# Attention and a squared-ReLU FFN on one core: the second FFN matrix product with seven block products in place of eight

## The chip, the cores and the metric

The kernel runs on one core of one Trainium2 chip. The metric is the device time of one execution in microseconds (us). TensorE (PE in the profile) multiplies, VectorE (DVE), ScalarE (ACT) and GpSimd (POOL) work element by element, and SyncE (SP) issues every DMA of this kernel.

## The reference

Eight batches, twelve heads, 448 positions, head size 64, all in float32. The attention output, 3584 rows of 768, goes through an FFN.

```python
q_n, k_n = rmsnorm(q, g_q), rmsnorm(k, g_k)
scores = q_n @ k_n.T / sqrt(64)
attn = softmax(scores) @ v              # per batch and head
x = attn as (3584, 768)
h = x @ w_in                            # w_in  (768, 2048), float64 in memory
g = s * relu(h) ** 2 + b
out = (g @ w_out).astype(float32)       # w_out (2048, 768), float64 in memory
```

## The kernel before

**Numbers in two parts.** TensorE takes its operands as fp32r. To keep float32 accuracy, each operand is held as a rounded part (hi) and a remainder (lo), and a product is three matmuls: hi by hi, hi by lo, lo by hi. The weights arrive as float64; L130 to L138 put the two 32-bit words of each number together into float32 with four DVE operations and one ACT square, and L141 and L144 split that into hi and lo.

**The attention loop** (L612 to L655) is written as slots. One slot (s_) handles one chunk of 128 keys of one head: `score_t` (2 matmuls), `score` for the chunk ten slots ahead (1 matmul, followed on DVE by `maximum`), `weigh` for the chunk two slots behind (3 matmuls, or 2 for the last chunk of a head). A pair of heads takes 8 slots, a batch 48. All engines get their instructions in exactly the order in which they are written. On DVE, `split_e_lo` (L453, tile al) of a slot must be done before `weigh` of the next slot starts; it also frees a PSUM bank that a later `score` (L375, tile sh) takes. Other work hangs on slot numbers in the table `jobs`: the norm (L317), scaling (L338), the divisor (L495) and so on of pairs to come.

**FFN1** (h = x w_in) runs inside this loop as filler: from slot START = 8 of the next batch on, six matmuls a slot, exactly 48 slots for the 288 matmuls of a batch. Its input tiles x are split in slots 7 to 12 of the batch (`split_x`, L517). What is left of the last batch runs after the loop, in the first part of FFN2's code (L722 to L753), 18 matmuls a step. There w_out is loaded, converted and split in 32 pieces (`load_double`, L120), into the room of w_in. The rectified h goes to DRAM (r_d).

**FFN2** (out = g w_out) has 28 tiles of 128 rows. `squares` (L672) loads a tile of h with all 2048 columns, squares it on ACT (L685), applies s and b on DVE (L686), and splits it (L690, L691). `ffn_out` (L694) runs 16 chunks times three matmuls times two column halves: 96 matmuls of 384 columns per tile (L703), 2688 in all, into two PSUM banks.

Of the kernel before, what the change touches and what calls it, by code (L numbers as in the profile page):

```python
# [20 lines left out]

LEAST = (1 + 1 / 8) * 2.0 ** (0x70 - 127)

START = 8

AHEAD = 10

# [6 lines left out]
TURNED = 10  # L34

PLAIN = 10

GAP = 2

# [2 lines left out]
def attention_then_relu2_ffn(  # L42
# [49 lines left out]
    NS = 4  # L92
    FS = DF // NS
    WI = 512
    WO = 384
    W = 8
    NSLOT = W * NPAIR

# [10 lines left out]
    warm = cpool.tile([P, 1], F32, name="warm")  # L109

    r_d = [dpool.tile([NFC, P, SEQ], F32, name=f"r_d{b}") for b in range(B)]
    z_d = [dpool.tile([2, SEQ], F32, name=f"z_d{p}") for p in range(NPAIR)]
    i_d = [dpool.tile([2, 2 * SEQ], F32, name=f"i_d{p}") for p in range(NPAIR)]

# [2 lines left out]
        bank = free.pop(0)  # L117
        return ps.tile([P, 512], F32, tag=bank, name=name), bank

    def load_double(room, dst_hi, dst_lo, src, apart=False, rest=None):  # L120

        w, words, m = room
        nc.sync.dma_start(w.rearrange("p n t -> p (n t)"), src)
        yield
        a = words()
# [9 lines left out]
        V.scalar_tensor_tensor(af, m.bitcast(F32), LEAST * LEAST, af, ALU.is_ge, ALU.mult)  # L138
        for _ in range(GAP):
            yield  # L140
        S.copy(dst_hi, af)  # L141
        if apart:
            yield
        (rest or G).tensor_tensor(dst_lo, af, dst_hi.bitcast(F32), ALU.subtract)  # L144
        yield

    w_in32 = w_in.bitcast(I32)
    w_out32 = w_out.bitcast(I32)
    whi, wlo, ohi, olo = ([None] * NS for _ in range(4))
# [12 lines left out]
    def parts_of_w_out():  # L162
        n = NFC // NS
        for i in range(NS):
            ohi[i] = wpool.tile([P, n, DM], F32R, tag=f"wh{i}", name=f"woh{i}")
            olo[i] = wpool.tile([P, n, DM], F32R, tag=f"wl{i}", name=f"wol{i}")
            for f in range(n):
                r0 = (i * n + f) * P
                for c0 in range(0, DM, WO):
                    c = slice(c0, c0 + WO)  # L170
                    src = w_out32[r0 : r0 + P, 2 * c0 : 2 * (c0 + WO)]
                    yield ohi[i][:, f, c], olo[i][:, f, c], src

# [43 lines left out]
    with tc.tile_pool(name="apool", bufs=1) as ap:  # L217
# [280 lines left out]
        def divide(p, step):  # L498
# [24 lines left out]
        def pieces():  # L523
            for i, (hi, lo, src) in enumerate(parts_of_w_in()):
# [38 lines left out]
        for p in range(NPAIR):  # L563
# [26 lines left out]
            at(s0 + 16, divide, p, 2)  # L590
            at(s0 + 18, divide, p, 3)
# [5 lines left out]
        for i, s_ in enumerate(PACE):  # L597
            for n in range(5):
                at(s_ + n, convert, i, n)
            at(s_ + 3, load_piece)  # L600

        def within(i):
            return 0 <= i < NSLOT
# [53 lines left out]
            keep_r()  # L657


    with tc.tile_pool(name="opool", bufs=2) as op:  # L660

        def pieces():
            for i, part in enumerate(parts_of_w_out()):
                w = op.tile([P, WO, 2], I32, tag="w64", bufs=4, name=f"w64o{i}")
                m = op.tile([P, WO], F32, tag="wm", bufs=2, name=f"wmo{i}")

                def words(i=i):
                    return op.tile([P, WO], I32, tag="wa", bufs=6, name=f"wao{i}")

                yield load_double((w, words, m), *part, apart=True, rest=V)  # L670

        def squares(t):  # L672
            r = op.tile([P, NFC, P], F32, tag="r2", bufs=2, name=f"r2_{t}")
            t0 = t * P
            while t0 < (t + 1) * P:
                b, off = divmod(t0, SEQ)
                n = min((t + 1) * P - t0, SEQ - off)
                o = t0 - t * P
                nc.sync.dma_start(
                    r[:, :, o : o + n],  # L680
                    r_d[b][:, :, off : off + n].rearrange("f p t -> p f t"),
                )
                t0 += n
            yield
            S.activation(r, r, AF.Square)  # L685
            V.tensor_scalar(r, r, sb_s, sb_b, ALU.mult, ALU.add)  # L686
            yield
            gh = op.tile([P, NFC, P], F32R, tag="gh", bufs=3, name=f"gh{t}")
            gl = op.tile([P, NFC, P], F32R, tag="gl", bufs=3, name=f"gl{t}")
            S.copy(gh, r)  # L690
            V.tensor_tensor(gl, r, gh.bitcast(F32), ALU.subtract)  # L691
            yield gh, gl

        def ffn_out(ts, gs):  # L694
            n = NFC // NS
            pos = [[psum(f"po{t}_{e}") for e in range(2)] for t in ts]
            for i in range(NS):
                for (gh, gl), po in zip(gs, pos):
                    for f in range(n):
                        fc = i * n + f  # L700
                        for m, (x, w) in enumerate(((gh, ohi[i]), (gh, olo[i]), (gl, ohi[i]))):
                            for e in range(2):
                                T.matmul(  # L703
                                    po[e][0][:, :HALF],
                                    x[:, fc, :],
                                    w[:, f, e * HALF : (e + 1) * HALF],
                                    start=fc == 0 and m == 0,
                                    stop=fc == NFC - 1 and m == 2,
                                )
            for t, po in zip(ts, pos):  # L710
                ot = op.tile([P, DM], F32, tag="ot", name=f"ot{t}")
                S.copy(ot[:, :HALF], po[0][0][:, :HALF])
                V.tensor_copy(ot[:, HALF:], po[1][0][:, :HALF])
                free.extend(bank for _, bank in po)
                nc.sync.dma_start(out[t * P : (t + 1) * P, :], ot)

        first = [squares(t) for t in range(3)]
        gs = []
        pieces = pieces()


        later_by = 2  # L722
        with tc.manual_schedule(engines=ORDERED - {ENGINE.SP}):
            waiting = []
            todo = list(islice(pieces, 2))
            for g in todo:
                next(g)
            for m in range(NFC + later_by):
                filler(NCC * 3)
                now, todo = todo, list(islice(pieces, 2))  # L730
                for g in todo:
                    next(g)
                if m in (1, 2, 3):
                    next(first[m - 1])
                old = waiting[:2] if m >= later_by else []
                waiting = waiting[len(old) :]
                for step in range(4):
                    for g in now:
                        next(g)
                    if step == 0:  # L740
                        rectify()
                        keep_r()
                        for g in old:
                            for _ in range(GAP):
                                next(g)
                    if step == 2:
                        for g in old:
                            next(g)
                waiting += now
                if m in (6, 8, 10):  # L750
                    next(first[(m - 6) // 2])
                if m in (7, 9, 11):
                    gs.append(next(first[(m - 7) // 2]))  # L753
        ffn_out([0, 1, 2], gs)
        for t in range(3, NT // P):
            *_, g = squares(t)
            ffn_out([t], [g])


_INS = ["moe_w_in", "moe_w_out", "moe_s", "moe_b"]  # L760
# [41 lines left out]
```

## Time and profile before

| | us |
|---|---|
| median of 3 runs | 1480.66 (1477.99 to 1481.07) |
| the profiled execution | 1479.64 |
| its span, first to last instruction | 1477.8 |
| PE busy, share of the span | 1443.6, 98% |
| DVE busy | 863.5, 58% |
| ACT busy | 799.8, 54% |
| POOL busy | 687.8, 47% |
| granted TensorE clock, mean | 0.994 of full speed |

Matmuls are pipelined, so a busy PE is not by itself a PE at its peak. The distance between the starts of matmuls tells how fast it goes. The execution has three stretches: an opening of about 217 us, in which PE often waits; the attention loop with filler up to about 955 us; and the FFN2 stretch, whose matmuls run from 1006 us to 1473 us.

### The profile page before, as it was taken

What the parts mean: (1) busy time and instruction counts of PE and PEld (TensorE: products, weight loads), DVE (VectorE), ACT (ScalarE), POOL (GpSimd) and SP (SyncE); (2) the same over time, 40 slices, a digit from 0 to 9 for tenths busy, and PEclk for the clock granted to TensorE, in tenths of its full rate; (3) what the DMA queues carried; (4) which work ended last, traced back from release to release, by engine and by line L of the source; (5) the groups of instructions that cost most, each with busy time, mean ns of one, the idle gap of its engine ahead of it and who ended that gap; (6) DMA issues with size and microseconds to landing.
All of it is one profiled execution on the core that took longest, in us unless ns stands there. A gap on an engine that the chain in (4) does not pass through costs nothing.

```text
span 1477.8 us, 21404 instructions
## 1 busy us (share of the span) xinstructions
PE 1443.6 (98%) x7360; PEld 1328.2 (90%) x7360; DVE 863.5 (58%) x1347; ACT 799.8 (54%) x1466; POOL 687.8 (47%) x559
## 2 busy tenths in 40 slices
PE   7998999999999999999999999999999999999998
PEld 5666779899899899899899999899999999999998
DVE  6888896766766766766676764289522222222210
ACT  5876566766766767766766766456332222222210
POOL 7797787777777767767777763100000000000000
PEclk8999999999999999999999999999999999999999
DMA  4545776666666666666666652288323323233200
GB/s 130 142 129 155 215 215 194 183 196 189 194 197 173 184 194 196 180 202 182 181 200 190 193 177 68 98 280 251 116 81 90 104 82 79 80 96 99 79 22 33
DMA packets 215100, 223.46 MB, mean 151 GB/s; under 512 B 75536, under 2 KB 192272, under 8 KB 214992
## 3 DMA queue, kind: packets, MB, share of 16 engines
q1 hardware_dynamic: 214992, 222.10, 51.4%
q8 instruction: 58, 0.95, 0.3%
q14 instruction: 50, 0.41, 0.1%
HBM read 169.87 MB, written 40.81 MB: 143 GB/s over the span
## 4 chain that ended last, share of the span: by engine, by line
PE 82%; DVE 8%; DMA 3%; issue 2%; POOL 2%; ACT 2%; SPq 0%; POOLq 0%; ACTq 0%; DVEq 0%
PE po L703 31%; PE ph L185 24%; PE av L472 13%; PE sh L375 5%; PE st L413 4%; PE st L416 4%; DMA w64o<-in_dram 1%; DMA w64i<-in_dram 1%; DVE nmx L386 1%; DVE kq L338 1%; PE tk L253 1%; DVE x L521 1%; DVE wao L133 1%; DVE ssq L317 1%; DVE al L453 1%
## 5 line engine op out<-in xcount | busy, mean ns | idle before, releaser
L185 PE MATMUL ph<-x,wih 128*128 128x448 f32 x1536 | 492.7, 367 | 5.6 <-ACT x L520 3.1
L185 PEld LDWEIGHTS ph<-x,wih 128*128 128x128 f32 x1536 | 288.5, 189 | 35.4 <-issue 5.3
L386 DVE TENSOR_REDUCE nmx<-sh 112x1 fp32r<-112x448 f32 x384 | 237.2, 620 | 114.0 <-PE sh L375 111.3
L185 PE MATMUL ph<-x,wil 128*128 128x448 f32 x768 | 291.1, 379 | 0.0
L432 ACT ACTIVATE st<-st 128x448 f32<-128x448 f32 (+1 forms) x304 | 159.4, 524 | 222.0 <-PE st L416 219.3
L703 PE MATMUL po<-woh,gh 128*128 128x384 f32 x896 | 227.6, 334 | 1.0 <-ACT gh L690 1.0
L703 PE MATMUL po<-woh,gl 128*128 128x384 f32 x896 | 227.4, 334 | 0.0
L703 PE MATMUL po<-wol,gh 128*128 128x384 f32 x896 | 227.3, 334 | 0.0
L472 PE MATMUL av<-ah,vs 128*128 128x448 f32 x608 | 173.9, 367 | 3.6 <-DVE al L453 3.6
L440 ACT CAST ah<-st 128x448 fp32r<-128x448 f32 (+1 forms) x304 | 162.6, 535 | 1.6
L703 PEld LDWEIGHTS po<-woh,gh 128*128 128x128 f32 x896 | 161.7, 188 | 1.4 <-ACT gh L690 1.3
L375 PE MATMUL sh<-ka,qa 128*112 128x448 f32 x384 | 147.9, 387 | 14.3 <-DVE ka L265 7.2
L703 PEld LDWEIGHTS po<-woh,gl 128*128 128x128 f32 x896 | 161.7, 188 | 0.1
L703 PEld LDWEIGHTS po<-wol,gh 128*128 128x128 f32 x896 | 161.6, 188 | 0.0
L453 DVE TENSOR_TENSOR al<-st,ah 128x448 fp32r<-128x448 f32 x228 | 139.6, 612 | 36.9 <-ACT ah L440 24.1
L185 PEld LDWEIGHTS ph<-x,wil 128*128 128x128 f32 x768 | 144.6, 188 | 16.5 <-issue 5.3
L413 PE MATMUL st<-qa,ka 128*128 128x448 f32 (+1 forms) x384 | 158.0, 411 | 1.0 <-ACT e L428 0.9
L685 ACT ACTIVATE r<-r 128x2048 f32<-128x2048 f32 x28 | 53.7, 1919 | 170.3 <-DMA r<-r_d 170.3
L513 POOL TENSOR_TENSOR u<-uz,zb 64x448 f32<-64x448 f32 x96 | 123.0, 1281 | 40.0 <-DMA zb<-z_d 36.4
L416 PE MATMUL st<-qb,kb 128*128 128x448 f32 (+1 forms) x384 | 140.8, 367 | 0.0
L686 DVE TENSOR_SCALAR r<-r,sb_s,sb_b 128x2048 f32<-128x2048 f32 x28 | 37.6, 1344 | 172.3 <-ACT r L685 172.3
L375 PEld LDWEIGHTS sh<-ka,qa 128*112 128x112 f32 x384 | 107.4, 281 | 27.0 <-issue 5.3
(75 smaller groups left out, 2120.5 us busy)
## 6 DMA issues: line engine op xcount, KB each, us to landing
kq<-in_dram SPq DMA_DIRECT2D x76, 448.0 KB, 5.1
rb<-i_d SPq DMA_DIRECT2D x76, 448.0 KB, 6.0
r_d<-r SPq DMA_DIRECT2D x128, 224.0 KB, 3.1
r<-r_d SPq DMA_DIRECT2D x24, 1024.0 KB, 5.9
raw<-in_dram SPq DMA_DIRECT2D x38, 448.0 KB, 5.0
w64i<-in_dram SPq DMA_DIRECT2D x24, 512.0 KB, 4.6
w64o<-in_dram SPq DMA_DIRECT2D x32, 384.0 KB, 4.4
kb<-ka SPq DMA_DIRECT2D x96, 112.0 KB, 2.9
```

The costliest lines, as they stand in the source:

```text
L185: T.matmul(ph[:, :SEQ], w[:, cc, f0 : f0 + P], xs[b, cc][:, part, :], start=cc == 0 and m == 0, stop=cc == NCC - 1 and m == 2,)
L375: T.matmul(sh[:QC, :SEQ], qa[p % 2][:, a].rearrange("k (p c) -> k c p", c=NQ)[:, c], ka[p % 2][:, a], start=True, stop=True,)
L386: V.tensor_reduce(out=nmxs[p][:, c : c + 1], in_=sh[:QC, :SEQ], op=ALU.max, axis=AX.X, negate=True)
L413: T.matmul(st[:rows, :SEQ], ka[n][:, keys], qa[n][:, q], start=True, stop=False)
L416: T.matmul(st[:rows, :SEQ], kb[n][:, keys], qb[n][:, q], start=False, stop=True,)
L432: S.activation(st[:rows, :SEQ], st[:rows, :SEQ], AF.Exp)
L440: S.copy(ah[:rows], sts[i][0][:rows, :SEQ])
L453: V.tensor_tensor(al, st[:rows, :SEQ], ah[:rows].bitcast(F32), ALU.subtract)
L472: T.matmul(av[:, :SEQ], x, a, start=kc == 0 and m == 0, stop=kc == 3 and m == len(todo) - 1,)
L513: G.tensor_tensor(u[a], uzs.pop((p, j))[a], zb[a], ALU.mult)
L685: S.activation(r, r, AF.Square)
L703: T.matmul(po[e][0][:, :HALF], x[:, fc, :], w[:, f, e * HALF : (e + 1) * HALF], start=fc == 0 and m == 0, stop=fc == NFC - 1 and m == 2,)
```

## The change

FFN2 is computed by Strassen's scheme in its form with 7 products. Two row tiles (256 rows), the two halves of the 2048 inner indices, and the two halves of the 768 columns form 2 by 2 blocks. Seven products of (128 x 1024) by (1024 x 384) replace eight; each is 24 matmuls of 384 columns. There are 14 groups of 7 products, 2352 matmuls. The left sums (`sum1` to `sum4`) and the output sums (`settle`) are made on DVE. The four right sums need w_out as float32 before it is split: in batches 2 to 7 of the attention loop, four pieces per batch, at slots 16, 24, 32 and 40 of the batch (`PACE_OUT`), are loaded, converted and summed, and the blocks (b_d) and sums (t_d) are written to DRAM. After the loop they are loaded in chunks and split in place. START goes from 8 to 9, the divisor of the last pair of a batch is one slot earlier (`soon`), and the tile u has 5 buffers, not 6.

```diff
-START = 8
+START = 9
+PACE_OUT = tuple(48 * b + 16 + 8 * i for b in range(2, 8) for i in range(4))
@@ the attention loop
-                u = us[p] = ap.tile([P, SEQ], F32, tag="u", bufs=NP, name=f"u{p}")
+                u = us[p] = ap.tile([P, SEQ], F32, tag="u", bufs=NP - 1, name=f"u{p}")
...
+        def load_out(i):
+            f, c = divmod(i, NQ3)
+            w = wides[i] = ap.tile([P, WI, 2], I32, tag="w64", bufs=2, name=f"w64o{i}")
+            to = w.rearrange("p (h e n) t -> p h e (n t)", h=2, e=2)
+            for h in range(2):
+                r0 = (h * NH + f) * P
+                src = w_out32[r0 : r0 + P].rearrange("p (e n) -> p e n", e=2)
+                nc.sync.dma_start(to[:, h], src[:, :, 2 * c * P : 2 * (c + 1) * P])
+        def convert_out(i, n):
+            if n == 0:
+                a, m = (
+                    ap.tile([P, WI], I32, tag="wa", bufs=2, name=f"wao{i}_{k}") for k in range(2)
+                )
+                singles[i] = to_single(wides.pop(i), a, m.bitcast(F32)), a, m
+            steps, a, m = singles[i]
+            if n < 4:
+                next(steps, None)
+                return
+            w = a.bitcast(F32).rearrange("p (h e n) -> p h e n", h=2, e=2)
+            t = m.bitcast(F32).rearrange("p (k n) -> p k n", k=4)
+            V.tensor_tensor(t[:, 0:2], w[:, :, 1], w[:, 0], ALU.subtract)
+            V.tensor_tensor(t[:, 2], w[:, 1, 1], t[:, 0], ALU.subtract)
+            V.tensor_tensor(t[:, 3], w[:, 1, 0], t[:, 2], ALU.subtract)
+        def keep_out(i):
...
+            for d, of in ((b_d, a), (t_d, m)):
+                nc.sync.dma_start(
+                    d[:, :, f, c * P : (c + 1) * P].rearrange("k p n -> p k n"),
+                    of.bitcast(F32).rearrange("p (k n) -> p k n", k=4),
+                )
...
-            at(s0 + 13, invert, p)
-            at(s0 + 14, divide, p, 1)
+            soon = 1 if p >= TURNED and p % NP == NP - 1 else 0
+            at(s0 + 13 - soon, invert, p)
+            at(s0 + 14 - soon, divide, p, 1)
...
+        for i, s_ in enumerate(PACE_OUT):
+            at(s_ - 4, load_out, i)
+            for n in range(5):
+                at(s_ + n, convert_out, i, n)
+            at(s_ + 6, keep_out, i)
@@ FFN2, in place of load_double's pieces, squares and ffn_out
+        def load_chunk(i):
...
+            nc.sync.dma_start(lo.bitcast(F32), d[n, :, 2 * c : 2 * c + 2])
+        def split_chunk(i):
...
+            S.copy(hi, lo.bitcast(F32))
+            V.tensor_tensor(lo, lo.bitcast(F32), hi.bitcast(F32), ALU.subtract)
...
+        def split(n):
...
+            S.copy(hi[0], single(u))
+            V.tensor_tensor(lo[0], single(u), single(hi), ALU.subtract)
+            release(u)
+        def multiply(n):
...
+            for f in range(NH):
+                for m, (a, w) in enumerate(((hi, whi_), (hi, wlo_), (lo, whi_))):
+                    T.matmul(
+                        po, a[:, f], w[:, f],
+                        start=f == 0 and m == 0, stop=f == NH - 1 and m == 2,
+                    )
...
+            splits = {1: 20, 2: 22, 4: 24, 5: 26}
+            loads = {0: 5, 3: 6}
+            for n in range(7 * NG):
+                g, k = divmod(n, 7)
+                if n in loads:
+                    for i in range(4):
+                        load_chunk(4 * loads[n] + i)
+                multiply(n)
+                if n:
+                    settle(n - 1)
+                if n > 1:
+                    split(n + 2)
+                if n in splits:
+                    for i in range(2):
+                        split_chunk(splits[n] + i)
+                if g + 1 < NG:
...
+                    if k in (2, 3):
+                        for c in QUADS[2 * k - 4 : 2 * k - 2]:
+                            square(g + 1, *c)
+                            affine(g + 1, *c)
```

On VectorE, in slots 4 and 5 of a pair of heads in the middle of a batch, this stood (ah and al are the remainders of the softmax numerators, nmx the maxima, ssq the norm's sum, kq the scaled keys):

```order
L453 TENSOR_TENSOR ah_5548<-st_5519,ah_5548 64x448
L386 TENSOR_REDUCE nmx_5398<-sh_5554 112x1
L317 TENSOR_REDUCE ssq_5573<-raw_5449 128x14
L338 SCALAR_TENSOR_TENSOR kq_1_5472<-kq_1_5472,gqk,rb_1_5474 128x448
L453 TENSOR_TENSOR al_5587<-st_5543,ah_5570 128x448
```

and now stands, where a piece of w_out is converted beside the pair (wao are its words):

```order
L445 TENSOR_TENSOR ah_6135<-st_6105,ah_6135 64x448
L378 TENSOR_REDUCE nmx_5978<-sh_6144 112x1
L564 TENSOR_TENSOR wao_1_6039<-wao_0_6038 128x256
L565 TENSOR_TENSOR wao_1_6039<-wao_0_6038,wao_1_6039 128x128
L566 TENSOR_TENSOR wao_1_6039<-wao_0_6038,wao_1_6039 128x128
L309 TENSOR_REDUCE ssq_6167<-raw_6030 128x14
L330 SCALAR_TENSOR_TENSOR kq_1_6057<-kq_1_6057,gqk,rb_1_6059 128x448
L445 TENSOR_TENSOR al_6183<-st_6130,ah_6164 128x448
```

Three subtractions come in ahead of ssq, kq and al; the other four conversion steps stand one each in slots 0 to 3.

On VectorE, in slots 12 and 13 of a batch, where FFN1 takes over the next x tiles, this stood:

```order
L521 TENSOR_TENSOR x_5_5789<-u_5729,x_5_5789 128x448
L453 TENSOR_TENSOR ah_5783<-st_5752,ah_5783 64x448
L386 TENSOR_REDUCE nmx_5619<-sh_5792 112x1
L317 TENSOR_REDUCE ssq_5811<-raw_5674 128x14
L338 SCALAR_TENSOR_TENSOR kq_1_5703<-kq_1_5703,gqk,rb_1_5705 128x448
L453 TENSOR_TENSOR al_5827<-st_5778,ah_5808 128x448
```

and now stands:

```order
L513 TENSOR_TENSOR x_4_5902<-u_5611,x_4_5902 128x448
L445 TENSOR_TENSOR ah_5896<-st_5865,ah_5896 64x448
L378 TENSOR_REDUCE nmx_5735<-sh_5908 112x1
L309 TENSOR_REDUCE ssq_5927<-raw_5782 128x14
L330 SCALAR_TENSOR_TENSOR kq_1_5816<-kq_1_5816,gqk,rb_1_5818 128x448
L513 TENSOR_TENSOR x_5_5937<-u_5811,x_5_5937 128x448
L445 TENSOR_TENSOR al_5944<-st_5891,ah_5924 128x448
```

Every x split is one slot later, so x_5 now stands in slot 13, behind ssq and kq and ahead of al.

On TensorE, at the seam of FFN1 (ph) and FFN2, this stood:

```order
L185 MATMUL ph_15_11444<-x_5_10859,wih_1993 128x448
L703 MATMUL po_0_11578<-woh_10885,gh_11249 128x384
L703 MATMUL po_1_11579<-woh_10885,gh_11249 128x384
L703 MATMUL po_0_11578<-wol_10886,gh_11249 128x384
L703 MATMUL po_1_11579<-wol_10886,gh_11249 128x384
```

and now stands:

```order
L177 MATMUL ph_15_11608<-x_5_11221,wih_1989 128x448
L802 MATMUL p_0_11666<-comb00h,roomh 128x384
L802 MATMUL p_0_11666<-comb00l,roomh 128x384
L802 MATMUL p_0_11666<-comb00h,rooml 128x384
L802 MATMUL p_0_11666<-comb00h,roomh 128x384
```

L703 stood 2688 times, L802 stands 2352 times; the matmuls have the same shape, and a product now fills one bank at a time.

## Rows read from the trace of the kernel before

**Rows 1.** Busy us by stretch: PE, PEld, DVE, ACT, POOL (instructions), granted clock, DMA share, GB/s.
```profile
144.00:217.00 73.00, 68.78 (x288) 55.60 (x288) 64.92 (x90) 43.47 (x85) 56.65 (x45) 0.95 0.72 213
...
424.00:540.00 116.00, 115.33 (x565) 105.25 (x564) 81.68 (x132) 81.11 (x166) 85.28 (x66) 1.00 0.66 191
...
955.00:1006.00 51.00, 51.00 (x254) 47.27 (x253) 44.36 (x95) 29.14 (x51) 0.00 (x0) 1.00 0.87 284
1006.00:1478.00 472.00, 466.18 (x2688) 465.46 (x2686) 141.62 (x150) 124.60 (x113) 0.00 (x0) 1.00 0.31 90
```

**Rows 2.** The same by stretch, instructions on FFN2's PSUM tile po alone.
```profile
1100.00:1200.00 100.00, 100.00 (x578) 100.00 (x578) 3.35 (x6) 2.80 (x6) 1.00 0.31 87
```

**Rows 3.** Timeline of PE at its waits: start us, us, instruction, [idle before <-releaser].
```profile
492.82 0.36 PE L185 MATMUL ph<-x,wil 128*128 128x448 f32 x1
493.55 0.56 PE L375 MATMUL sh<-ka,qa 128*112 128x448 f32 x1 [0.37 <-DVE al L453]
...
508.24 0.56 PE L185 MATMUL ph<-x,wih 128*128 128x448 f32 x2
509.10 0.67 PE L472 MATMUL av<-ah,vs 128*128 128x448 f32 x2 [0.30 <-DVE al L453]
...
953.07 0.47 PE L185 MATMUL ph<-x,wih 128*128 128x448 f32 x1 [0.33 <-ACT x L520]
...
1018.35 0.62 PE L703 MATMUL po<-woh,gh 128*128 128x384 f32 x2 [1.00 <-ACT gh L690]
```

**Rows 4.** Timeline of DVE in slots 4 and 5 of a pair.
```profile
446.37 1.08 DVE L317 TENSOR_REDUCE ssq<-raw 128x14 f32<-128x896 f32 x1 [0.18 <-ACT raw L312]
...
447.96 0.62 DVE L453 TENSOR_TENSOR al<-st,ah 128x448 fp32r<-128x448 f32 x1
```

**Rows 5.** Timeline of PE in slots 6 of that pair and 2 of the next.
```profile
449.85 0.36 PE L375 MATMUL sh<-ka,qa 128*112 128x448 f32 x1
...
450.46 0.57 PE L472 MATMUL av<-ah,vs 128*128 128x448 f32 x2
...
459.43 0.36 PE L375 MATMUL sh<-ka,qa 128*112 128x448 f32 x1
```

**Rows 6.** Instructions by tile: duration ns min/median/max, first and last start.
```profile
L130 DVE TENSOR_SCALAR wai<-w64i x24: 375/418/2204, 9.8 to 214.4; 128x512 int32<-128x512 int32 x24
L133 DVE SCALAR_TENSOR_TENSOR wai<-w64i,wai x24: 691/693/2777, 10.3 to 214.9; 128x512 int32<-128x512 int32 x24
...
L144 DVE TENSOR_TENSOR wol<-wao,woh x32: 537/541/554, 967.9 to 1040.8; 128x384 fp32r<-128x384 f32 x32
...
L703 PEld LDWEIGHTS po<-wol,gh x896: 187/188/188, 1005.9 to 1472.3; 128*128 128x128 f32 x180
...
L691 DVE TENSOR_TENSOR gl<-r,gh x28: 2273/2293/2294, 996.0 to 1424.9; 128x2048 fp32r<-128x2048 f32 x28
...
L686 DVE TENSOR_SCALAR r<-r,sb_s,sb_b x28: 1329/1347/1349, 990.4 to 1401.8; 128x2048 f32<-128x2048 f32 x28
...
L338 DVE SCALAR_TENSOR_TENSOR kq<-kq,gqk,rb x67: 674/676/1298, 216.5 to 856.4; 128x448 f32<-128x448 f32 x67
```

**Rows 7.** Timelines of SP, ACT, DVE around slot 0 of the next pair.
```profile
451.85 0.54 SPq L215 DMA_DIRECT2D r_d<-r  x1
...
455.08 0.53 ACT L440 CAST ah<-st 128x448 fp32r<-128x448 f32 x1
456.98 0.53 ACT L432 ACTIVATE st<-st 128x448 f32<-128x448 f32 x1 [1.36 <-PE st L416]
...
456.27 0.62 DVE L453 TENSOR_TENSOR al<-st,ah 128x448 fp32r<-128x448 f32 x1
```

**Rows 8.** DMA issues: queue, count, KB each, median us from issue to landing.
```profile
r_d<-r SPq DMA_DIRECT2D x128, 224.0 KB, 3.1
r<-r_d SPq DMA_DIRECT2D x24, 1024.0 KB, 5.9
```

**Rows 9.** Timeline of DVE at the x tile of slot 7 of a batch.
```profile
492.33 0.63 DVE L521 TENSOR_TENSOR x<-u,x 128x448 fp32r<-128x448 f32 x1 [2.86 <-ACT x L520]
```

More of the change, by code (lines that the diff above doesn't have):

```diff
@@ L94, in attention_then_relu2_ffn @@
     WI = 512
-    WO = 384
+    NH = NFC // 2
+    NQ3 = HALF // P
     W = 8
@@ L111, in attention_then_relu2_ffn @@
     r_d = [dpool.tile([NFC, P, SEQ], F32, name=f"r_d{b}") for b in range(B)]
+    b_d = dpool.tile([4, P, NH, HALF], F32, name="b_d")
+    t_d = dpool.tile([4, P, NH, HALF], F32, name="t_d")
     z_d = [dpool.tile([2, SEQ], F32, name=f"z_d{p}") for p in range(NPAIR)]
@@ L118, in psum, with to_single @@
         return ps.tile([P, 512], F32, tag=bank, name=name), bank
[L120 to L128, printed above, removed]
+    def to_single(w, a, m):
         low, high = w[:, :, 0], w[:, :, 1]
@@ L138, in load_double @@
         V.scalar_tensor_tensor(af, m.bitcast(F32), LEAST * LEAST, af, ALU.is_ge, ALU.mult)
+    def load_double(room, dst_hi, dst_lo, src):
+        w, words, m = room
+        nc.sync.dma_start(w.rearrange("p n t -> p (n t)"), src)
+        yield
+        a = words()
+        yield from to_single(w, a, m)
         for _ in range(GAP):
             yield
[L141 to L144, printed above, removed]
+        S.copy(dst_hi, a.bitcast(F32))
+        yield
+        G.tensor_tensor(dst_lo, a.bitcast(F32), dst_hi.bitcast(F32), ALU.subtract)
         yield
@@ L148, in attention_then_relu2_ffn @@
     w_out32 = w_out.bitcast(I32)
-    whi, wlo, ohi, olo = ([None] * NS for _ in range(4))
+    whi, wlo = ([None] * NS for _ in range(2))
     def parts_of_w_in():
@@ L657, in attention_then_relu2_ffn, with half, unit, release @@
             keep_r()
[L660 to L675, printed above, removed]
+    with tc.tile_pool(name="opool", bufs=1) as op:
+        def half(pool, tag, shape, name):
+            return pool.tile(shape, F32R, tag=tag, name=name)
+        ALL = (
+            (op, "c0", b_d, 0), (op, "c1", b_d, 2), (wpool, "0", t_d, 2), (wpool, "1", t_d, 0),
+            (wpool, "2", t_d, 1), (wpool, "3", b_d, 3), (op, "c2", t_d, 3),
+        )
+        room = [half(op, f"c2{x}", [P, 3, NH, P], f"room{x}") for x in "hl"]
+        spare = {k: tuple((r[:, k], None) for r in room) for k in range(3)}
+        units = [f"un{i}" for i in range(6)]
+        combs = {}
+        def unit(name):
+            tag = units.pop(0)
+            return (xp if tag[0] == "x" else op).tile([P, NH, P], F32R, tag=tag, name=name), tag
+        def release(*us):
+            units.extend(tag for _, tag in us if tag is not None)
+        def load_chunk(i):
+            k, c = divmod(i, 4)
+            pool, tag, d, n = ALL[k]
+            if c == 0:
+                names = (f"wh{tag}", f"wl{tag}") if pool is wpool else (f"{tag}h", f"{tag}l")
+                combs[k] = [half(pool, x, [P, NH, HALF], f"comb{k}{x[-2:]}") for x in names]
+            lo = combs[k][1][:, 2 * c : 2 * c + 2]
+            nc.sync.dma_start(lo.bitcast(F32), d[n, :, 2 * c : 2 * c + 2])
+        def split_chunk(i):
+            k, c = divmod(i, 4)
+            hi, lo = (x[:, 2 * c : 2 * c + 2] for x in combs[k])
+            S.copy(hi, lo.bitcast(F32))
+            V.tensor_tensor(lo, lo.bitcast(F32), hi.bitcast(F32), ALU.subtract)
+        NG = NT // (2 * P)
+        As = [{} for _ in range(NG)]
+        halves = {}
+        def single(u):
+            return u[0].bitcast(F32)
+        def load_a(g, t, h):
+            u = As[g][t, h] = unit(f"a{g}_{t}_{h}")
+            t0 = first = (2 * g + t) * P
+            while t0 < first + P:
@@ L682, in squares @@
                 )
                 t0 += n
[L684 to L728, printed above, removed]
-                filler(NCC * 3)
[L730 to L757, printed above, removed]
+        def square(g, t, h):
+            a = single(As[g][t, h])
+            S.activation(a, a, AF.Square)
+        def affine(g, t, h):
+            a = single(As[g][t, h])
+            V.tensor_scalar(a, a, sb_s, sb_b, ALU.mult, ALU.add)
+        def combine(g, to, x, y, op_):
+            A = As[g]
+            if to == 3:
+                u = A.pop((1, 0))
+                V.tensor_tensor(single(u), single(x), single(u), op_)
+            else:
+                u = unit(f"s{g}_{to}")
+                V.tensor_tensor(single(u), single(x), single(y), op_)
+            A[to] = u
```

124 lines of the change are left out of this document (105 added, 19 removed).

## The prediction

> **What bounds the kernel now.** Read the busy time by stretch first [rows 1]: from the middle of the loop on, PE is busy in about 99% of every stretch, at a granted clock of 1.00 (2.4 GHz), DVE in 70% of the loop (81.68 of 116 us), ACT in 70%, POOL in 74%. A batch of the loop makes 565 matmuls in 116 us, 205 ns each; FFN1's rest 254 in 51 us, 201 ns; FFN2 578 in 100 us [rows 2], 173.0 ns. No other engine shows in FFN2: DVE 142 and ACT 125 of 472 us. So from about 217 us on the time is a count of matmuls, plus the places where PE waits. Those are the second view [rows 3]: twice at the start of a batch, behind al on DVE; once behind the last x tile (953.07); once in FFN2 behind the split of its third left tile (1018.35). Only the opening is not bound so: 288 matmuls in 73 us.
>
> **FFN2: what is removed.** 2688 - 2352 = 336 matmuls of the same shape go. At 173.0 ns that is **-58.1 us**. A product now fills one bank at a time and changes the loaded operand in two matmuls of three. FFN1's rest does both already, with a change at every matmul: its 201 ns for 448 columns stand 14 above the 187 that 448 columns take at 2.4 GHz, FFN2's 173 for 384 stand 13 above 160. So I keep 173.0. The Trainium skill, page "TensorE: Matmul & The Clock Gate", section "Back-to-back issue gap", gives columns over 2.4 GHz plus 2.5 ns for a warm clock; for 384 columns that would be an estimate of 162.5 ns and a saving of 54.6 us. The trace has 173.0, and that decides.
>
> **What FFN2 asks of DVE and ACT.** The subtractions took 541 ns for 384 columns and 2293 for 2048 [rows 6], a line of 0.137 us plus 1.053 ns a column: 1.215 us for 1024. A group of 7 products needs 4 affine steps (half of 1347 ns, 0.67 each), 4 sums and 7 remainders (1.215 each) and 8 output sums of 384 columns (0.54, like wol): 2.7 + 13.4 + 4.3 = 20.4 us of DVE in 168 x 0.173 = 29.1 us of PE. ACT has 11 copies and squares of 1024 columns, at most 1.2 each by 0.53 for 448 [rows 7]: 13 us. Each `split` stands two products, 8.3 us, ahead of its use, so PE waits for nothing once this runs: 0. The first group has also the last chunks of the weights to split, 8 x 0.945 us, in products 1, 2, 4 and 5. In products 2 to 5 DVE then has 5.0, 4.2, 6.0 and 5.4 us against 4.15 each, and the last two chunks come about when product 6 wants them. Bounds 0 and 4.2 us (all of the excess); I take **+1.0**. The wait of 1.00 us at 1018.35 goes: the first left parts are made in steps 6, 7 and 10 of the 14 FFN1 steps, when DVE no longer converts w_out: **-1.0**. What is late there next is the chunk load, two steps ahead of its splits; a step lasts 18 x 0.201 = 3.6 us, and loads of 1 MB land in 5.9 us [rows 8].
>
> **The loop: 24 pieces of w_out.** A piece costs DVE 0.418 + 3 x 0.69 ([rows 6]; the two steps not shown taken like L133) and three subtractions of 256, 128 and 128 columns, 0.41 + 0.27 + 0.27 = 0.95: 3.4 us, 13.8 a batch on 81.7 of 116. On ACT it is one square of 512 columns, 0.6 us by 0.53 for 448 [rows 7]. Average room is no proof; the tightest place is. In slots 4 and 5 of a pair DVE does ssq, kq and al, and al ends at 448.58 [rows 4]; the PE instructions that may need it are sh at 449.85 and av at 450.46 [rows 5]. So al has 1.27 us of cover. The subtractions go in just ahead, 0.95 less the 0.18 in which ssq waits for ACT: 0.77, which leaves 0.5. The four other steps stand one a slot in slots 0 to 3, where the cover is twice that (al of 456.27 ends at 456.89, the sh behind it is at 459.43 [rows 5, 7]). Each piece alone then costs PE nothing. Between 0 and 0.95 us a piece I take 0.1 for pieces that meet another delay: **+2.4**, bounds 0 and 22.8.
>
> A second wait is added. The tiles wa have two buffers and a piece now uses both, so the next piece's first step (DVE) and its square (ACT) wait until the stores of b_d and t_d have landed. The stores are written after kb in slot 6, where SP stood at 451.85 [rows 7]; the second is out at about 452.4. Stores of 224 KB landed in 3.1 us, 1 MB in small rows in 5.9 [rows 8]; these have 256 KB. At 3.1 the square starts at 455.5, and behind it on ACT is ah, which began at 455.08 and would be 1.1 late; al on DVE began at 456.27 only, so it is 0.5 late against a cover of 2.54. At 5.9 it would be 3.3 late, 0.8 over the cover, in 18 pieces (those with one 8 slots ahead): 14 us. I take 3.1, nearest in size, so 0 here, and keep 14 as a bound. The exponents behind ah idle 1.36 us in such a slot, which takes up the rest.
>
> **START 9.** At a batch's start, x_0 stood in slot 7, where ACT has two other casts ahead of it and DVE waited 2.86 us [rows 9]; in slot 8 it has not, so the wait of 493.55 (0.53 against a step of 0.20 from 492.82) goes. But x_5 moves into slot 13, ahead of the al that PE waits for at 509.10 (0.46 late), and adds its 0.62. Per batch -0.53 + 0.62, six batches: **+0.5**, bounds -5.9 (both waits gone) and +3.7. One slot less of filler stands in the opening, where PE waits anyway, and six matmuls more run alone at the end: 6 x 0.201 = **+1.2**, bounds -2 and +1.2. The last pair's divisor is two slots earlier against the x tile, so the wait at 953.07 goes: **-0.3**. The fifth buffer of u makes POOL wait for x_0, one slot before; the x_5 that it feeds is four slots on: 0.
>
> **The sum.** -58.1 + 1.0 - 1.0 + 2.4 + 0.5 + 1.2 - 0.3 = -54.3 us on the profiled execution's own 1479.64, which is 1.0 below the median of the runs: 1425.3. **Forecast 1425 us.** With every bound favourable: -58.1 - 1.0 - 5.9 - 2 - 0.3 = -67.3, 1412.
>
> **Rivals.** *A slower loop.* The added steps do reach PE: the stores land late (14), or the subtractions pass on whole (22.8 in place of 2.4), or half of each. For it: DVE goes to 82% and DMA, already at 66%, carries 1 MB more per piece; pieces of w_in beside the loop had steps of 693 ns that took up to 2777 [rows 6]. Against: the covers above, and kq in the loop took 676 ns at the median and 1298 at most. Price 11 to 34, about **1441**. The Trainium skill, page "SBUF — State Buffer", section "SBUF: two separate sides", says that a DVE instruction with two SBUF inputs and a POOL instruction exclude each other for their whole length. By that rule each of a piece's six such steps would wait for half a POOL instruction in 74% of cases (66 in 85.28 us, 1.29 each), an estimate of 0.5 us a step; the three subtractions would then run 1.5 us later, pass the 0.5 us that is left by 1.0, and cost 24 us, the same rival. The trace bears it out in part: the maximum of 2777 does, the median of 676 does not.
>
> *The load floor.* A weight load takes 188 ns [rows 6] and is hidden at 173 now, where two matmuls in a row always have the same operand loaded. If a changed operand made the load the pace, 2352 x 0.015 = 35 us come back: **1460**. Against it: FFN1's rest.
>
> *The left parts come late: slower than before.* If a `split` could begin only when its product is due (a buffer that is freed too late, an SP load behind a waiting store), ACT's copy and DVE's remainder and output sum, 1.2 + 1.2 + 0.5 = 2.9 us, would stand bare in each of 97 products: +281, **1706**. It decides from 58 / 97 = 0.6 us a product. Against it: the two products of lead, and 12 buffers handed round.
>
> *A better seam.* Both waits at batch starts go and the opening gains a slot: **1415**.
>
> **How the numbers follow.** Forecast (1416 to 1433) 0.66; slower loop (1434 to 1447) 0.20; load floor or some of it (1448 to 1475) 0.05; slower than before 0.03; better seam 0.05; within 0.2% of before 0.01. The range 1414 to 1442 holds the forecast, most of the better seam and half of the slower loop. A measurement of this kernel can tell about 0.2% from no change. Faster by more than that: 0.96, within it 0.01, slower 0.03.
>
> **What would show it.** L802 at 173 ns a start and 2352 times, FFN2's matmuls over 407 us; a batch of the loop at 116 us as before, with no PE wait in slots 5 to 7 of a pair; the wait of slot 8 gone and one in slot 14 of about 1.1 us; no wait of PE for a split in FFN2 after the first group. The forecast is wrong if the batches 2 to 7 are each over 118 us (then ACT's square waits for DMA, or al is late after the subtractions), or if L802's starts are over 180 ns apart.

## The result and the profile after

The changed kernel takes **1440.39 us** (median) against 1480.55 for the kernel before: ratio **0.9731**, 95% interval 0.9712 to 0.9750. The profiled execution took 1440.49 us, its span 1438.7. One execution of the four, with no trace, took 4856.58 us for a reason that stays open; the ratio leaves it out, and the other three lie within 0.7 us. The forecast was 1425 with a range of 1414 to 1442: the direction and the range held, the likeliest value was 15 us too low. The time fell into the band of the rival "a slower loop", though not by that rival's mechanism; the range held because it took in half of that band, which is luck.

The first view is again the busy time by stretch (columns as in [rows 1]): a stretch of the opening, one batch of the loop, all of FFN2, and then 100 us of FFN2 on its PSUM tile alone, as in [rows 2].

```profile
144.00:217.00 73.00, 68.60 (x288) 55.72 (x289) 63.72 (x90) 42.42 (x84) 56.88 (x44) 0.95 0.70 207
424.00:540.00 116.00, 114.34 (x559) 104.10 (x559) 92.77 (x159) 82.56 (x169) 90.85 (x66) 1.00 0.77 223
...
1023.00:1436.00 413.00, 409.88 (x2354) 409.23 (x2352) 268.31 (x304) 165.01 (x170) 0.00 (x0) 1.00 0.37 102
...
1100.00:1200.00 100.00, 100.00 (x579) 100.00 (x578) 13.85 (x25) 1.44 (x3) 1.00 0.33 90
```

FFN2 is what was forecast, but for one stall in its first group (below): 2352 matmuls, 579 in 100 us where it was 578, PE without a gap in that stretch, DVE with 268 of 413 us. In the loop DVE rose from 81.68 to 92.77 us of 116 and DMA from 0.66 to 0.77, and PE fell from 565 matmuls to 559. That is small in a row that averages a batch, so the next step is to mark where each stage starts in the trace (the first matmul of slot 0, of slot 96, of slot 383, of FFN2, the last of FFN2, the end):

| stretch, us | before | after | difference | forecast |
|---|---|---|---|---|
| up to slot 96 | 240.65 | 241.25 | +0.6 | 0 |
| slots 96 to 383, first 16 slots of six batches | 237.62 | 251.07 | **+13.45** | +0.5 |
| slots 96 to 383, all other slots | 455.24 | 456.57 | +1.3 | +2.4 |
| from slot 383 to FFN2 | 72.21 | 74.30 | +2.1 | +0.9 |
| FFN2, first to last matmul | 467.13 | 411.75 | -55.4 | -58.1 |
| after the last matmul | 4.99 | 3.77 | -1.2 | 0 |
| sum | 1477.84 | 1438.71 | -39.1 | -54.3 |

So nearly all of the shortfall stands in 16 slots of 48: the batch starts. PE's waits from the loop to the first group of FFN2 (engine line <- releaser: us in total, times, longest):

```profile
PE ph L177 <- DVE x L513: 10.2, 7, 1.7
PE p L802 <- DVE comb62l L729: 2.4, 1, 2.4
PE sh L367 <- DVE ah L445: 0.7, 2, 0.5
PE av L464 <- DVE al L445: 0.7, 2, 0.3
```

Before, the waits were for al [rows 3]; now six batch starts wait 1.65 us each for an x tile. One of them closely, in the timelines of PE, DVE and POOL (start us, us, instruction, [idle before <-releaser]), slots 13 and 14 of a batch:

```profile
394.17 0.36 PE L367 MATMUL sh<-ka,qa 128*112 128x448 f32 x1
396.18 0.68 PE L177 MATMUL ph<-x,wih 128*128 128x448 f32 x2 [1.65 <-DVE x L513]
...
392.94 1.08 DVE L309 TENSOR_REDUCE ssq<-raw 128x14 f32<-128x896 f32 x1
393.94 0.72 DVE L330 SCALAR_TENSOR_TENSOR kq<-kq,gqk,rb 128x448 f32<-128x448 f32 x1
394.58 1.55 DVE L513 TENSOR_TENSOR x<-u,x 128x448 fp32r<-128x448 f32 x1
396.05 0.61 DVE L445 TENSOR_TENSOR al<-st,ah 128x448 fp32r<-128x448 f32 x1
...
394.14 1.51 POOL L329 TENSOR_TENSOR kq<-kq,rb 128x448 f32<-128x448 f32 x1
```

x_5 stands behind ssq and kq on DVE, as the prediction said. But it takes 1.55 us and not 0.62: it began while POOL's half of the kq scaling ran, and ended 0.48 us after that half (395.65 to 396.13). In the kernel before, the same row had x_5 ahead of ssq, in slot 12, at its bare length, and DVE's kq began 0.17 us ahead of POOL's:

```profile
504.96 0.62 DVE L521 TENSOR_TENSOR x<-u,x 128x448 fp32r<-128x448 f32 x1 [0.54 <-ACT x L520]
...
507.81 0.70 DVE L338 SCALAR_TENSOR_TENSOR kq<-kq,gqk,rb 128x448 f32<-128x448 f32 x1
508.43 0.61 DVE L453 TENSOR_TENSOR al<-st,ah 128x448 fp32r<-128x448 f32 x1
...
507.98 1.53 POOL L337 TENSOR_TENSOR kq<-kq,rb 128x448 f32<-128x448 f32 x1
```

The second cost follows the wait. By stretch, the granted clock (the column before the last two) after that wait and after the one in FFN2:

```profile
396.00:398.00 2.00, 1.82 (x8) 1.38 (x9) 1.97 (x7) 0.97 (x2) 1.92 (x2) 0.91 0.04 8
398.00:401.20 3.20, 3.20 (x10) 2.75 (x9) 1.68 (x3) 2.23 (x5) 1.97 (x2) 0.52 0.21 38
401.20:404.60 3.40, 3.40 (x18) 3.16 (x18) 2.18 (x5) 1.60 (x4) 2.30 (x3) 1.00 0.76 219
1053.00:1056.40 3.40, 3.40 (x11) 3.40 (x12) 3.40 (x4) 0.00 (x0) 0.00 (x0) 0.50 0.07 21
```

From about 397.6 to 401.1 the clock is at the lower of its two levels, 1.2 GHz, and matmuls of 448 columns start 0.37 us apart where 0.20 to 0.21 is the rule: 1.5 us more in all. That happened after three of the six waits of this execution: those batch starts took 42.3 to 42.9 us, the others 40.8 to 41.4.

In FFN2 the one stall, PE and DVE:

```profile
1050.23 0.34 PE L802 MATMUL p<-comb62h,hi 128*128 128x384 f32 x1
1052.96 0.69 PE L802 MATMUL p<-comb62l,hi 128*128 128x384 f32 x1 [2.39 <-DVE comb62l L729]
1053.45 0.52 PE L802 MATMUL p<-comb62h,lo 128*128 128x384 f32 x1
...
1048.63 1.22 DVE L766 TENSOR_TENSOR s<-s,a 128x1024 f32<-128x1024 f32 x1
1049.77 0.55 DVE L834 TENSOR_TENSOR o0a<-p,o0a 128x384 f32<-128x384 f32 x1
1050.35 0.56 DVE L837 TENSOR_TENSOR o0d<-p,o0a 128x384 f32<-128x384 f32 x1
1050.83 1.21 DVE L789 TENSOR_TENSOR lo<-a,hi 128x1024 fp32r<-128x1024 f32 x1
1051.96 1.82 DVE L729 TENSOR_TENSOR comb62l<-comb62l,comb62h 128x768 fp32r<-128x768 f32 x2
```

The seventh product of the first group wants the third chunk of its weights at 1050.4; DVE, without a gap since 1042.3, splits it behind two output sums and a left part that were needed later.

### The profile page after: what moved, and what is told of

It reads as the page before. It is cut to its first block, busy times and chain, and to the rows that moved or that the text cites. A ratio compares the mean times of both kernels' runs of the same rounds, so it can differ in the third digit from the quotient of the medians.

```text
span 1438.7 us, 21357 instructions
## 1 busy us (share of the span) xinstructions
PE 1396.9 (97%) x7024; PEld 1276.0 (89%) x7024; DVE 1056.8 (73%) x1607; ACT 852.6 (59%) x1538; POOL 724.6 (50%) x559
## 4 chain that ended last, share of the span: by engine, by line
PE 86%; DVE 6%; issue 2%; ACT 2%; DMA 2%; POOL 1%; SPq 0%; DVEq 0%; ACTq 0%; POOLq 0%
PE ph L177 30%; PE p L802 28%; PE av L464 13%; PE sh L367 5%; PE st L405 5%; PE st L408 5%; DVE nmx L378 1%; DVE x L513 1%; PE tk L245 1%; DVE kq L330 1%; DMA zt<-uz 1%; DMA w64i<-in_dram 1%; DVE wai L128 0%; DVE wai L131 0%; DVE wai L133 0%
## 5 line engine op out<-in xcount | busy, mean ns | idle before, releaser
L505 POOL TENSOR_TENSOR u<-uz,zb 64x448 f32<-64x448 f32 x96 | 142.1, 1480 | 68.0 <-DMA zb<-z_d 62.3
L464 PE MATMUL av<-ah,vs 128*128 128x448 f32 x608 | 174.8, 369 | 0.7 <-DVE al L445 0.7
L445 DVE TENSOR_TENSOR al<-st,ah 128x448 fp32r<-128x448 f32 x228 | 139.0, 610 | 15.3 <-ACT ah L432 11.3
L351 POOL TENSOR_TENSOR ka<-kq,ka 64x448 fp32r<-64x448 f32 x76 | 103.0, 1355 | 46.2 <-ACT ka L348 39.5
L464 PEld LDWEIGHTS av<-ah,vs 128*128 128x128 f32 x608 | 113.6, 189 | 13.5 <-DVE al L445 3.9
L788 ACT CAST hi<-a 128x1024 fp32r<-128x1024 f32 x54 | 56.7, 1051 | 87.2 <-PE p L802 71.7
L352 POOL TENSOR_TENSOR qb<-kq,qa 64x448 fp32r<-64x448 f32 x76 | 99.7, 1311 | 5.7
L329 POOL TENSOR_TENSOR kq<-kq,rb 128x448 f32<-128x448 f32 x76 | 102.2, 1345 | 0.5
L313 POOL TENSOR_TENSOR ri<-ri,mhalf 128x14 f32<-128x14 f32 x38 | 98.8, 2600 | 3.2
L298 POOL TENSOR_TENSOR vs<-vr,vs 128x512 fp32r<-128x512 f32 x38 | 56.3, 1482 | 80.2 <-issue 76.1
L197 ACT ACTIVATE r<-ph 128x448 f32<-128x448 f32 x128 | 69.7, 545 | 42.0 <-PE ph L177 27.3
```

Of the source, the lines that this page charges most:

```text
L351: G.tensor_tensor(ka[n][D:, a], t[D:, 0], ka[n][D:, a].bitcast(F32), ALU.subtract)
L445: V.tensor_tensor(al, st[:rows, :SEQ], ah[:rows].bitcast(F32), ALU.subtract)
L464: T.matmul(av[:, :SEQ], x, a, start=kc == 0 and m == 0, stop=kc == 3 and m == len(todo) - 1,)
```

## The experiments

**Place or load.** Theory P: the batch starts, that is START = 9. Theory L: the pieces. Three runs part them.

> The changed kernel with START = 8 as in the kernel before: FFN1 8 slots behind, the six splits of x in slots 7 to 12, everything else as changed. Theory P (place): the 14.8 us by which the attention loop grew stand at the batch starts, where x_5, now split in slot 13 behind ssq and kq, comes 1.8 us late. It expects the six batch starts to give back about 2 us each, 12 to 13 us in all: 1427 to 1429 us, against 1440.4. Theory L (load): the loop grew because the 24 pieces of w_out load VectorE, ScalarE, SyncE and the DMA engines, and START does not matter. It expects no more than 2 us of difference: 1438 to 1442.

```diff
-START = 9
+START = 8
```

Measured 1429.44 us (0.9661, 0.9647 to 0.9675), 11 us less than the changed kernel: theory P, 0.4 us above its band. Three of its batch starts take 39.6 us as before, three still 41.04 (batches 3, 5 and 7).

> The kernel before with START = 9 and nothing else: FFN2 in eight products, no pieces of w_out in the loop, the splits of x in slots 8 to 13. Theory P (place): slower by about 2 us at each batch start after which the FFN1 weights are there, 10 to 14 us in all: 1491 to 1495 us, against 1480.6. Theory L (load): within 2 us of the kernel before, 1479 to 1482.

```diff
-START = 8
+START = 9
```

Measured 1491.93 us (1.0085, 1.0066 to 1.0104), P again; the profiled execution is the longest of its four, 1495.81. Its waits and the row of DVE and POOL are those of the changed kernel, without any piece in the loop:

```profile
PE ph L185 <- DVE x L521: 9.9, 6, 1.7
...
635.86 1.54 DVE L521 TENSOR_TENSOR x<-u,x 128x448 fp32r<-128x448 f32 x1
...
635.41 1.51 POOL L337 TENSOR_TENSOR kq<-kq,rb 128x448 f32<-128x448 f32 x1
```

Its six batch starts grew by 13.4 us in the profiled execution, three at 42.6 us and three at 41.07; the three longer ones hold the half clock.

> The kernel before with the 24 pieces added to its loop (loads, conversion, three subtractions, stores to the two intermediate tensors) and nothing else: FFN2 stays in eight products and doesn't read what the pieces wrote. Theory P (place): 1 to 3 us slower than before, 1481 to 1484 us, the growth in slots 16 to 47 of the batches. Theory L (load): 10 to 15 us slower, 1490 to 1496.

```diff
...
+        for i, s_ in enumerate(PACE_OUT):
+            at(s_ - 4, load_out, i)
+            for n in range(5):
+                at(s_ + n, convert_out, i, n)
+            at(s_ + 6, keep_out, i)
```

Measured 1482.49 us (1.0017, 1.0007 to 1.0026): 2.2 us for 24 pieces. The batch starts stay at 39.6. DVE and DMA are as full as in the changed kernel, and PE does not mind:

```profile
424.00:540.00 116.00, 115.33 (x564) 104.94 (x563) 95.37 (x163) 82.95 (x170) 91.80 (x67) 1.00 0.77 227
```

Theory L is out.

**The stall of FFN2.**

> The changed kernel with the seventh product's part of w_out split earlier: its last two chunks stand ahead of the fifth product's settling on VectorE, the seventh product takes its low part last, and the eighth takes the low part of its sum last. Theory D (VectorE's order): the one stall of FFN2, 2.5 us at 1052.96, is a split that stood behind three other steps of VectorE, and the half clock of the 3.4 us behind it goes with it: 3 to 4 us faster than the changed kernel, 1436.4 to 1437.4 us. Theory M (transfers): the chunk was late because its load was, and VectorE's order changes nothing beyond 0.5 us: 1440.

```diff
...
+                if n == 5:
+                    split_chunk(26)
+                    split_chunk(27)
                 if n:
                     settle(n - 1)
...
-                if n in splits:
+                if n in splits and n != 5:
```

In code that is not shown, the seventh product also takes its terms as hi·hi, lo·hi, hi·lo, each over all chunks, and the eighth as hi·hi, hi·lo, lo·hi. Measured 1436.56 us (0.9708, 0.9688 to 0.9728), 3.8 less than the changed kernel: theory D. Its executions range from 1433.57 to 1440.22, so the proof is the stage and not the total. PE waits nowhere in its FFN2, which takes 407.5 us from first to last matmul where the changed kernel took 411.75, and the chunks now come first (what the earlier split and the new order of terms each give was not parted):

```profile
1048.29 1.81 DVE L729 TENSOR_TENSOR comb62l<-comb62l,comb62h 128x768 fp32r<-128x768 f32 x2
1050.02 0.55 DVE L836 TENSOR_TENSOR o0a<-p,o0a 128x384 f32<-128x384 f32 x1
```

**What makes x_5 late: its place, or POOL.**

> The changed kernel with START = 9 and x_5 in slot 13 as they are, and GpSimd's half of the kq scaling (line 329) one slot later, so that in slot 13 GpSimd computes nothing beside x_5; VectorE's half stays where it is. Theory S (VectorE stands still while GpSimd's step runs): x_5's step falls from 1.55 to 0.62 us, PE's wait in slot 14 from 1.8 to 0.9 us, and with the shorter wait the half clock behind it may stay away: 6 times 0.9 us and 0 to 4 us, 1431 to 1435 us. Theory T (only the row's order on VectorE counts, its step is long for another reason): 1439 to 1442.

```diff
-            G.tensor_tensor(t[:, 0], t[:, 0], rb[:, 0], ALU.mult)
             V.scalar_tensor_tensor(t[:, 1], t[:, 1], gqk, rb[:, 1], ALU.mult, ALU.mult)
+            yield
+            G.tensor_tensor(t[:, 0], t[:, 0], rb[:, 0], ALU.mult)
```

Measured 1435.59 us (0.9700, 0.9685 to 0.9714), 4.8 less, 0.6 above the band of theory S. The step itself did just what S said; POOL has nothing from 394.16 but ri, and PE waits less than half as long:

```profile
393.93 0.71 DVE L329 SCALAR_TENSOR_TENSOR kq<-kq,gqk,rb 128x448 f32<-128x448 f32 x1
394.56 0.61 DVE L514 TENSOR_TENSOR x<-u,x 128x448 fp32r<-128x448 f32 x1
...
392.85 1.31 POOL L298 TENSOR_TENSOR vs<-vr,vs 128x512 fp32r<-128x512 f32 x1 [2.36 <-issue]
394.24 0.47 POOL L312 TENSOR_SCALAR ri<-ssq 128x14 f32<-128x14 f32 x1
...
395.23 0.68 PE L177 MATMUL ph<-x,wih 128*128 128x448 f32 x2 [0.71 <-DVE x L514]
```

No half clock followed any of these six shorter waits; the batch starts fell by 5.9 us in all. Part of it came back: POOL's later step holds up other slots (four waits of 0.9 to 1.4 us away from slot 14).

> The changed kernel with START = 9 kept and one split moved: x_5 in slot 12, behind x_4, and no longer in slot 13 behind ssq and kq. Theory Q (its place in VectorE's row): what START = 9 costs is the wait of PE in slot 14 for x_5 alone; with x_5 a slot earlier nearly all that START = 8 gave back (11.0 us) comes back at START = 9 too: 1428 to 1432 us. Theory R (the later batch start as such, all six splits and FFN1 one slot on): 1438 to 1441.

```diff
-                at(W * NP * (b + 1) + START - 1 + g, split_x, b, g)
+                at(W * NP * (b + 1) + START - 1 + min(g, 4), split_x, b, g)
```

Measured 1432.4 us (0.9679, 0.9660 to 0.9699): most of what START = 8 gives, so theory R is out, and 0.4 us past the band of Q. PE no longer waits for x_5, but there is a new wait of 1.1 us in the same slot, for al. Now DVE's kq is the step that begins just behind POOL's half (0.13 us) and is held:

```profile
392.66 1.50 DVE L330 SCALAR_TENSOR_TENSOR kq<-kq,gqk,rb 128x448 f32<-128x448 f32 x1
394.08 0.61 DVE L445 TENSOR_TENSOR al<-st,ah 128x448 fp32r<-128x448 f32 x1
...
392.53 1.15 POOL L329 TENSOR_TENSOR kq<-kq,rb 128x448 f32<-128x448 f32 x1
...
394.75 0.67 PE L464 MATMUL av<-ah,vs 128*128 128x448 f32 x2 [1.09 <-DVE al L445]
```

**The two causes together, and the third.**

> START = 8 and the earlier last chunks of w_out together, on the changed kernel. If the two causes are separate, their gains add: 1440.4 less 11.0 and less 3.8, 1425 to 1426.5 us. If the stall of FFN2 hangs on when FFN1 ends, it comes back elsewhere: 1428 to 1429.5.

```diff
-START = 9
+START = 8
...
+                if n == 5:
+                    split_chunk(26)
+                    split_chunk(27)
...
```

Measured 1428.63 us (0.9654, 0.9640 to 0.9670), which neither theory names rightly. FFN2 kept its gain (407.5 us, no wait), but the batch starts took 7.4 us above 6 × 39.6, where the run with START = 8 alone took 4.4. Something else delays them, differently from start to start. In the run with START = 8 alone, batch 3, DVE in slots 4 and 5:

```profile
370.54 0.17 DVE L487 TENSOR_SCALAR zt<-zt 128x7 f32<-128x7 f32 x1 [2.00 <-DMA zt<-uz]
...
370.86 1.05 DVE L309 TENSOR_REDUCE ssq<-raw 128x14 f32<-128x896 f32 x1
371.83 0.90 DVE L330 SCALAR_TENSOR_TENSOR kq<-kq,gqk,rb 128x448 f32<-128x448 f32 x1
```

This is invert, which `soon` moved one slot forward: it waits for the transfer of the row sums, with ssq and kq behind it.

> The same as the run with START = 8 and the earlier chunks, and the last head pair of a batch normalized in the slots of the kernel before (the one slot that the change took from it given back, soon = 0). With START = 8 three of the six batch starts still take 41.04 us for 16 slots instead of 39.60. Theory U (VectorE's row): the earlier invert, in slot 4, waits 2.0 us for the row sums' transfer with ssq and kq behind it on VectorE; without it all six take 39.6 us, and 3 times 1.44 us go: 1421 to 1422.5 us. Theory V (the stores of the last piece before a batch start slow its transfers, wherever invert stands): no gain, 1425 to 1426.5.

```diff
-START = 9
+START = 8
...
-            soon = 1 if p >= TURNED and p % NP == NP - 1 else 0
+            soon = 0
...
+                if n == 5:
+                    split_chunk(26)
+                    split_chunk(27)
...
```

Measured **1423.03 us** (0.9613, 0.9598 to 0.9628): theory U, 0.5 above its band. All six batch starts take 39.59 to 39.61 us, and the 5.6 us to the run before are more than the 4.3 expected. The edit also puts back the store behind invert; that invert is what matters is read from the row above, not shown apart. What is left of PE's waits from the loop through FFN2's first group is near that of the kernel before:

```profile
PE av L464 <- DVE al L445: 2.7, 8, 0.6
PE sh L367 <- DVE al L445: 2.2, 6, 0.4
PE ph L177 <- ACT x L512: 0.4, 1, 0.4
```

This version is faster than both kernels, by 57 and by 17 us.

> The changed kernel with START = 9 and only the one early slot of a batch's last head pair given back (soon = 0). It parts the two causes at START = 9. Theory W (the split of x_5 is nearly all of it): the kernel before with START = 9 alone grew by 12.4 us in its six batch starts, the changed kernel by 13.5; giving the slot back brings about 1 us, 1438.5 to 1441 us. Theory X (each costs its own): it brings as much as at START = 8, where it was worth 5.6 us: 1434 to 1436.

```diff
 START = 9
...
-            soon = 1 if p >= TURNED and p % NP == NP - 1 else 0
+            soon = 0
```

Measured 1437.6 us (0.9711, 0.9697 to 0.9725). The total lies a little below W's band, but its batch starts are 13.5 us above 6 × 39.6, as much as in the changed kernel (13.45) and in the kernel before with START = 9 (13.4 by its rows; the 12.4 of the expectation was added up wrongly). So at START = 9 the earlier invert costs the loop nothing more: W. The 2.8 us are elsewhere: FFN2 took 2.05 us less, its stall being followed by no half clock, and FFN1's rest 1.2 less, its matmuls starting 203 ns apart and not 207.

> START = 9 with x_5 in slot 12, soon = 0 and the earlier last chunks, to be compared with the same at START = 8 (1423.0 us). The prediction gave START = 9 a gain of 0.5 us a batch start, the wait in slot 8. Theory Y (that gain is there once VectorE's row is calm): the first 16 slots of a batch take 39.0 to 39.1 us for 39.6, 1419 to 1421 us. Theory Z (with the splits a slot later the row of slot 13 still ends late, and the product with the exponentials waits there instead, 1.25 us as with x_5 moved alone): 40.4 us for 16 slots, 1427 to 1429.

```diff
 START = 9
...
+            soon = 0
...
+                at(W * NP * (b + 1) + START - 1 + min(g, 4), split_x, b, g)
...
+                if n == 5:
+                    split_chunk(26)
+                    split_chunk(27)
...
```

Measured 1430.38 us (0.9657, 0.9638 to 0.9676): theory Z, though 1.4 above its band. The wait is the one of the run with x_5 moved alone, `PE av L464 <- DVE al L445`, 7.6 us, 1.1 at the longest, and 16 slots take 40.9 us. START = 9 is 7 us dearer than START = 8 even with the rest in order.

## Why the range held and the likeliest value did not, point by point

- **FFN2's matmuls, -58.1: right.** 173 ns a start, 2352 of them; without its stall FFN2 takes 407.5 us, as the prediction said. The load floor (188 ns) did not appear, nor did left parts come late.
- **The wait for the first left parts, -1.0: right.** It is gone.
- **First group, +1.0 with bounds 0 and 4.2: mis-sized.** It cost 4.2: 2.5 of wait and the half clock behind it. That this equals the upper bound is an accident, for that bound was all of DVE's excess (4.0 by the prediction's own figures) and held no clock; in three other traces with a stall of 1.6 to 2.0 us and no half clock behind it FFN2 took 409.4 to 409.8 us, some 2 more than without a stall. The step that failed is "the last two chunks come about when product 6 wants them": the excess of DVE was summed by product, and the order within a product, which puts the chunk last, was not followed.
- **Pieces, +2.4: right.** 2.2 us by their own run, and 2.2 in the loop of the best version. The exclusion of DVE and POOL that the rival named does reach the pieces: of the three subtractions the first took 0.75 to 0.92 us in 18 of 24 pieces, where 0.42 is its length, ending 0.28 us after a POOL step each time, and the second 1.13 in place of 0.29 in four; the cover held all the same, as the 2.2 us show. The added wait for the stores is there (ACT's square waits 17.8 us in 16 pieces, 3.3 at the longest) and stays under cover: the stores landed in 2.6 and 3.0 us, near the 3.1 that was taken. The rival "slower loop" came out at its price by accident; its cause is excluded by the run that holds the pieces alone.
- **START 9, +0.5 with bounds -5.9 and +3.7: this step failed.** 13.4 us: 1.5 at each of six starts, and 1.5 more at the three with the half clock. Three parts of it were wrong. First, x_5 was priced at 0.62, its bare length, and as a delay of al; it took 1.55, and the matmul that reads x_5 itself stood ahead of al's reader. The wait in slot 14 of "about 1.1 us" that the prediction named among its signs is the 0.46 for al that stood before and this 0.62; what came is 1.65 for x_5. Second, the wait of slot 8 went, and in the kernel before with START = 9 it only moved into slot 9 (0.30 us, six times). Third, no term stood for a clock that falls behind a wait: 1.5 us in three starts. The upper bound counted none of the three.
- **The last pair one slot earlier: a term that was missing.** The prediction followed it to the x tile, and gave it -0.3 for the wait at 953.07. That wait is still there (0.34 us at 965.23). What else the step passes on its engines was not asked: invert moved ahead of ssq and kq on DVE. At START = 8 that costs 5.6 us; at START = 9 it costs the loop nothing that shows beside the larger loss.
- **One slot more of FFN1 alone, +1.2: right.** The rest of FFN1 grew by 2.1 in this execution, but some 1.2 of that is not tied to the change: its matmuls started 207 ns apart, as in two other traces (one of them with START = 8), and 203 apart in the kernel before and eight more, at a granted clock of 1.00 in both. At 203 ns the five other traces with START = 9 took 0.8 to 1.0 more than the kernel before. What sets the pace is open.
- **Not forecast:** the tail is 1.2 us shorter, of which 0.7 lies within what the tail of the old FFN2 varies by (4.3 in two other traces); that the rest comes of a last output 384 columns wide and not 768 was not tested. The opening differed by 0.6, within what it varies by (239.8 to 243.6 us up to slot 96 in these traces).

Of the signs that were named, the 173 ns of L802 and the end of the wait in slot 8 came. A batch took 117.8 to 119.6 us and not 116: three of the five that can be measured whole passed the 118 from which the prediction called itself wrong, but for neither of the two reasons that it gave.

With START = 8 and the pair's slot restored, and the chunk in time, the kernel takes 1423.0 us. The prediction's sum without its terms for START 9 (+0.5 and +1.2), the first group (+1.0) and the pair (-0.3) gives 1422.9, counted from the profiled execution, which is 1.0 below the median: it was right for the parts that the change is about, and wrong for what its schedule does.

## What to carry to other kernels

A step that is moved costs the length that it has beside its new neighbours, not the length that it had: look up what the other engine on the same memory runs at that moment, and who reads the step's result first. Follow every instruction of a moved chain, the small ones too: an instruction that waits for a transfer stops all that stands behind it on its engine. When a stretch is without slack, price a wait of a microsecond or two with what the clock may do behind it, and sort a burst on a busy engine by who needs it first.

## What the hardware did that was not expected

**DVE and POOL exclude each other.** In the changed kernel's loop, 12 of the 36 x steps of batches 2 to 7 began inside POOL's kq half; their median was 1.55 us against 0.62, and each of the 12 ended 0.48 us after POOL's instruction. Steps that were first kept their length, and then POOL's ended late: in the kernel before kq took 0.70 and POOL's half 1.53, against 1.15 where POOL's came first (392.53 in the run with x_5 moved). Steps with one operand in PSUM never showed it: al and ah took 0.57 to 0.63 us in all of some 290 cases, inside and outside POOL's instructions. The Trainium skill, page "SBUF — State Buffer", section "SBUF: two separate sides", says that whichever of a DVE step with two SBUF inputs and a POOL step that reads SBUF starts first holds the shared ports for its whole instruction while the other is blocked; the trace agrees in both directions. But the recorded start does not always tell who holds them: four x steps of the changed kernel (265.19 is one) began 0.53 us inside a POOL step on u, right behind a kq that was first, kept their 0.62 us, and POOL's step took 2.15; at 394.58 x_5 also stood right behind such a kq, and POOL's step came between. What decides there is open. One of the four, DVE and POOL:

```profile
264.60 0.67 DVE L330 SCALAR_TENSOR_TENSOR kq<-kq,gqk,rb 128x448 f32<-128x448 f32 x1
265.19 0.62 DVE L513 TENSOR_TENSOR x<-u,x 128x448 fp32r<-128x448 f32 x1
...
264.67 2.15 POOL L505 TENSOR_TENSOR u<-uz,zb 64x448 f32<-64x448 f32 x1
```

The prediction had weighed the rule against the pieces, by an average, and found it borne out in part; it was not asked where it hurt, in one row of a batch start. A difference of 0.3 us in who starts first (DVE's kq 0.17 us ahead in the kernel before, 0.13 behind with x_5 moved) made that step 0.8 us longer.

**A short wait can cost twice.** Of 24 waits of 1.65 us at batch starts (four executions with START = 9, x_5 in slot 13 and POOL's step in its place), 11 were followed by some 3 us at 1.2 GHz, 13 were not; nor were two of 1.68 us in the run with START = 8 and the earlier chunks. Of the stalls of 1.6 to 2.4 us in FFN2, two of five were. Behind waits of 0.9 to 1.4 us, 22 in these traces, there was none. Why one wait of 1.65 us brings it and the next does not is open; no run here tells it.
